# Padding the right-hand pools by 32 bytes, and asking for the next pair's halves and output splits earlier

## The chip, the cores and the metric

The kernel runs on one core of a Trainium2 chip. The metric is device time in microseconds (us) of one launch. The engines named below are PE (matrix products; it loads a stationary operand and streams a moving one past it), ACT and DVE (elementwise work, both can read the PSUM accumulators), POOL (elementwise work on SBUF) and SP, whose queue issues all the transfers here. Each engine and the SP queue work strictly in the order of their own instruction lists.

## The reference

Three layers in a row on 2304 tokens (4 batches of 576), width 512, all in float32:

```python
scores = scale * np.matmul(q, k.transpose(0, 1, 3, 2))
ret = scores * Dmat[None, :, :, :]
x = np.matmul(ret, v)                        # then heads side by side: (2304, 512)
h = x @ w_in                                 # 512 -> 2048
g = np.maximum(h, 0.0) + alpha * np.minimum(h, 0.0)
x2 = g @ w_out                               # 2048 -> 512
gate = 1.0 / (1.0 + np.exp(-(x2 @ w_gate)))  # 512 -> 1536
y = gate * (x2 @ w_val) @ w_out2             # 1536 -> 512
```

## The kernel before

Every float32 operand of a large product is split into a high and a low part (`split`: ACT writes the high part, then DVE the low part), and one product is three matmuls: high by high, high by low, low by high (`products`, line 562). A matmul of 512 columns is the unit of PE's work; "a group of 12" below is four such products, or two of the factored ones.

The tokens are cut into block 0 (256 tokens) and blocks 1 to 4 (512 each). The stages on PE's list, which is written by hand and is in program order:

- **Retention and layer 2 of block 0**, with the first `h` of block 1, up to about 152 us of the span; the weights are made from 64-bit words by ACT, DVE and POOL at the same time.
- **Layer 2 of blocks 1 to 4**, up to about 507 us: for each of 16 slices `f`, `ffn1_h` makes `h` (12 matmuls, stationary a slice of `w_in`, moving the tile `x`), ACT and DVE make `g` of it, and `ffn1_y` adds 12 matmuls into `y`. `h` has two accumulators, so `h` of slice f+2 needs `g` of slice f to be done. In block 4 the factors of pair 0 are made beside it (`left_factors(0, i)` at f = 7 and 10).
- **Layer 3 for pairs of blocks**, (1, 2) and then (3, 4): `z_step(n, t)` for t = 0 to 5 uses seven factored products (names a, b, c, e) with quarter weights `tq` as the stationary operand and factors `xf` as the moving one; each step is 14 products of 6 matmuls. Then `o_phase(n, r)` for the two blocks of the pair: 12 steps `i`, each splits one gated tile into `pp`, and multiplies it with an output weight `wo` (12 matmuls). The order of the steps is f = 0, 6, 1, 7, 2, 8, 3, 9, 4, 10, 5, 11. Pair 0's two phases make o1 and o2, pair 1's make o3 and o4. While o1 and o2 run, `left_factors(1, i)` for i = 0 and 1 makes pair 1's factors: it loads two halves `x2` (four transfers), POOL makes two sums and differences `s` of them, and seven splits make `xf1_*`.
- **Block 0 through layer 3** in plain form, from about 882 us.

The order of ACT, DVE, POOL and SP is not written by hand: a scheduler with a timeline of its own sets it, so that work which the program writes later can stand ahead of work written earlier.

Most tiles live in slots of 4096 bytes a partition, a line from which the oldest free one is taken (`slot`, `free`). Two pools lie on the right side of SBUF: `xp` (the tiles `x`, the moving operand of `h`) and, in the same place after layer 2 is done, `wide` with eight slots:

```python
xp = x_only.enter_context(tc.tile_pool(name="xp", bufs=2, side="right"))
...
pool = ctx.enter_context(tc.tile_pool(name="wide", bufs=1, side="right", reuse_waits="tile"))
spare.extend((pool, f"wide{i}") for i in range(NWIDE))
quarter_slots.extend(spare.pop() for _ in range(NQ))
```

The quarter weights have 14 slots of their own: the first seven were taken from the left side (f = 13 of block 4), the last seven are those of `wide`. They are used in turn, seven to a step, so the steps t = 0, 2, 4 read `tq` from the left side and t = 1, 3, 5 from the right. The eighth slot of `wide` goes into the common line.

Of the kernel before, what the change touches and what calls it, by code (L numbers as in the profile page):

```python
# [10 lines left out]
F32 = mybir.dt.float32  # L11
F32R = mybir.dt.float32r
# [7 lines left out]
P = 128  # L20
# [3 lines left out]
DM = 512  # L24
# [14 lines left out]
PAIRS = ((1, 2), (3, 4))  # L39
# [63 lines left out]
def retention_two_ffn(ctx: ExitStack, tc: tile.TileContext, att, cst, alpha, w1, w2, out):  # L103
    nc = tc.nc
# [8 lines left out]
    ps_a = ctx.enter_context(tc.tile_pool(name="ps_a", bufs=1, space=PSUM))  # L113


    x_only = ctx.enter_context(ExitStack())
    xp = x_only.enter_context(tc.tile_pool(name="xp", bufs=2, side="right"))
    att_only = ctx.enter_context(ExitStack())
# [16 lines left out]
    x2d = [dp.tile([P, KC, nb], F32, tag=f"x2d{j}", name=f"x2d{j}") for j, nb in enumerate(BLOCKS)]  # L135
# [9 lines left out]
    def slot(shape, dtype, name, line=spare):  # L145
        where = pool, tag = line.popleft()
        t = pool.tile(shape, dtype, tag=tag, name=name)
        held[t.tensor.name] = [where, 1, line]
        return t

    def free(t):
        h = held[t.tensor.name]
        h[1] -= 1
        if not h[1]:
            where, _, line = held.pop(t.tensor.name)
            line.append(where)
# [22 lines left out]
    def split(hi, lo, src, first=False):  # L179

        a = nc.scalar.activation(hi, src, AF.Copy)  # L181
        d = nc.vector.tensor_tensor(out=lo, in0=src, in1=hi.bitcast(F32), op=ALU.subtract)  # L182
        if first:
            urgent["act"].append(a)
            urgent["dve"].append(d)
# [55 lines left out]
    def fetch(f, m):  # L241
        if RES <= f < NF1 and (f, m) not in wt:
            wt[f, m] = slot([P, 2, DM], F32R, f"v{f}_{m}")
            uses[f, m] = 1
            nc.sync.dma_start(out=wt[f, m].bitcast(F32), in_=w1d[f, m])
# [84 lines left out]
    def second_pace(every):  # L330
        second_step()
        due[0] += 1
        if due[0] >= every:
            due[0] = 0
            begin_job()
        elif due[0] >= every - 2:
            ask()
# [164 lines left out]
    def runs_of(j):  # L502
        return [n for n, ch in enumerate(CHUNKS) if ch[0] == j]
# [6 lines left out]
    def att_stages(j):  # L510

        for n in runs_of(j):
            x_of(n)
            s_sb = att_scores(n, ps_a, "ab")
            load_qk(n + 1)
            yield
            att_values(n, s_sb, ps_a, "ab")
            load_kv(n + 1)
            if n + 1 < len(CHUNKS):
                att_q(n + 1)  # L520
                att_v(n + 1)
            yield
# [46 lines left out]
    def ffn1_h(j, f):  # L569
        w = weight(f, 0)  # L570
        nb = BLOCKS[j]
        ps = ps_h.tile([P, nb], F32, tag="h", name=f"h{j}_{f}")
        products(ps, [(cols(w, k), x_t[j][:, :, k]) for k in range(KC)])
        used(f, 0)
        t = small.tile([P, nb], F32, tag="t", name=f"t{j}_{f}", bufs=1)
        nc.scalar.activation(t, ps, AF.Relu)  # L576
        nc.scalar.activation(ps, ps, AF.Relu, scale=-1.0)  # L577
        nc.vector.scalar_tensor_tensor(ps, ps, na_sb[:, f:f + 1], t, ALU.mult, ALU.add)  # L578
        name = f"g{j}_{f}"
        g_t[j, f] = slot([P, 2, nb], F32R, name) if nb > DM // 2 else half_of_slot(name)  # L580
        split(g_t[j, f][:, 0], g_t[j, f][:, 1], ps, True)
# [41 lines left out]
    quarters = {}  # L623
    gated = {}

    def left_factors(n, i):

        a, b = [slot([P, 2, DM], F32, f"x2_{n}_{k}") for k in (i, i + 2)]
        for k, t in ((i, a), (i + 2, b)):
            for e, j in enumerate(PAIRS[n]):  # L630
                nc.sync.dma_start(out=t[:, e], in_=x2d[j][:, k, :])
        u, v = [slot([P, 2, DM], F32, f"s{n}_{i}_{c}") for c in range(2)]
        add = lambda o, x, y, op: nc.gpsimd.tensor_tensor(out=o, in0=x, in1=y, op=op)
        add(u[:, 0], a[:, 1], b[:, 1], ALU.add)
        add(u[:, 1], u[:, 0], a[:, 0], ALU.subtract)
        add(v[:, 0], a[:, 0], a[:, 1], ALU.subtract)
        add(v[:, 1], b[:, 0], u[:, 1], ALU.subtract)
        for m, src in ((1, a[:, 0]), (5, u[:, 0]), (6, u[:, 1]), (2, b[:, 0]), (7, v[:, 0]), (3, v[:, 1]), (4, b[:, 1])):
            x = factors[m, i] = slot([P, 2, DM], F32R, f"xf{n}_{m}_{i}")
            split(x[:, 0], x[:, 1], src)  # L640
        for t in (a, b, u, v):
            free(t)

    PLACE = {1: (0, 0), 5: (0, 1), 2: (1, 0), 6: (1, 1), 3: (2, 0), 7: (2, 1)}

# [2 lines left out]
    def load_quarters(t):  # L648
        need(t, 0)
        need(t, 1)  # L650
        for k in (0, 3, 1, 4, 2, 5, 6):
            w = quarters[t, k] = slot([P, 2, 2, 2, P], F32R, f"tq{t}_{k}", quarter_slots)
            nc.sync.dma_start(out=w.rearrange("p a i h j -> p a (i h j)").bitcast(F32), in_=td[t][k])
# [68 lines left out]
    def load_outer(f):  # L722
        need(f)
        outer[f] = slot([P, 2, DM], F32R, f"wo{f}")
        nc.sync.dma_start(out=outer[f].bitcast(F32), in_=wod[f])

    def second_y(ps, j, g, f, first, last):
        w = outer[f]
        for e, t in enumerate(ps):
            products(t, [(cols(g, e), w)], first, last)  # L730
            if last:
                r = FIRST[j] + e * P
                drain(e, f"ost{j}_{e}", t, out[r:r + P, :])

    ORDER2 = [f + c * NSTEP for f in range(NSTEP) for c in range(2)]

    def o_phase(n, r, between):
        j = PAIRS[n][r]
        ps = [
            pool.tile([P, DM], F32, tag=tag, name=f"o{j}_{tag}")  # L740
            for pool, tag in [(ps_y, "y")] * 2 + ([(ps_a, "a"), (ps_a, "b")] if r else [(ps_h, "h")] * 2)
        ]
        for i, f in enumerate(ORDER2):
            if i == 0:
                load_outer(ORDER2[0])
                load_outer(ORDER2[1])
            if i + 2 < NF2:
                load_outer(ORDER2[i + 2])
            g = slot([P, 2, DM], F32R, f"pp{j}_{f}")
            split(g[:, 0], g[:, 1], gated[f][:, r])  # L750
            second_y(ps, j, g, f, i == 0, i == NF2 - 1)
            free(g)
            free(outer.pop(f))
            if r:
                free(gated.pop(f))
            between(i)
# [49 lines left out]
    done = [0]  # L806
# [8 lines left out]
    def later(n):  # L815

        while len(late) > n:
            ffn1_y(*late.pop(0))
# [24 lines left out]
    n = runs_of(2)[0]  # L843
# [3 lines left out]
    for j in range(1, NBLK):  # L847
        stages = att_stages(j + 1) if j + 1 < NBLK else iter(())
        first = step1 if j == 1 else 0
        total = 2 * len(runs_of(j + 1))  # L850
        span = SPAN * (NF1 - first) // NF1
        staged = 0
        if j == NBLK - 1:

            for x in "ab":
                ps = ps_a.tile([P, DM], F32, tag=x, name=f"whole{x}")
                nc.tensor.matmul(ps, wt[0, 0][:, 0, :P], x_t[j][:, 0, 0], start=True, stop=True)
            att_only.close()
            pool = ctx.enter_context(tc.tile_pool(name="late", bufs=1, reuse_waits="tile"))
            spare.extend((pool, f"late{i}") for i in range(NLATE))  # L860
        for f in range(first, NF1):
            fetch(f, 0)
            fetch(f + 1, 0)
            fetch(f, 1)
            ffn1_h(j, f)
            if j > 1:
                second_pace(PACE_T[j == NBLK - 1])
            if j == NBLK - 1:
                if f in (7, 10):
                    left_factors(0, f // 10)  # L870
                if f == 13:
                    quarter_slots.extend(spare.popleft() for _ in range(NQ))
                    load_quarters(0)
            for point in range(2):
                if staged < total and staged * span < total * (2 * (f - first) + point):
                    next(stages)
                    staged += 1
                if point == 0:
                    later(BEHIND - 1)
            late.append((j, f))  # L880
        for _ in stages:
            pass
# [5 lines left out]
    def in_z(n, t):  # L888
# [7 lines left out]
            second_step()  # L896
        return between

    def in_o(n, r):
        def between(i):  # L900
            if n + 1 < len(PAIRS):
                if i == (1, 4)[r]:
                    left_factors(n + 1, r)
                if r == 1 and i == 6:
                    load_quarters(0)
            elif r == 1 and i == 2:
                load_x0()
        return between
# [14 lines left out]
    for f in range(NF2):  # L923
# [3 lines left out]
        g = plain_z(f, ws.pop(f))  # L927
# [51 lines left out]
```

## Time and profile before

| what | value |
|---|---|
| median of 3 runs | 940.03 us (938.67 to 940.82) |
| profiled execution, own time | 939.09 us |
| its span, first to last instruction | 937.2 us |
| PE busy | 898.6 us, 96% |
| DVE, ACT, POOL busy | 470.7, 404.9, 120.6 us |
| mean granted clock of PE | 0.989 |

The profiled execution's own time is 1.9 us over its span and 0.9 us under the median. A share is an average over the stages named above; the stretches are read one by one in the rows below. A busy PE need not be at its best rate, so the rows of equal work are compared with each other too.

### The profile page before, as it was taken

To read this page: it belongs to the slowest core of one execution; us is meant where nothing else is said; L and a number is where in the kernel's file an instruction comes from. 1 tells how busy PE (TensorE), PEld (TensorE's weight loads), DVE (VectorE), ACT (ScalarE), POOL (GpSimd) and SP (SyncE) were. 2 spreads that over 40 slices of the span, in tenths; PEclk is the share of its full clock that TensorE was granted. 3 is DMA by queue.
4 is the path that set the end of the run, shared out by engine and by line. 5 is a ranking of instruction groups with operands and counts; after the bars stand their busy time and mean duration, and the time that the engine had idled before them with its cause. 6 is when DMAs were issued, how large, how long until landed. Compare 5 with 4: busy or idle time off the path is not lost.

```text
span 937.2 us, 13173 instructions
## 1 busy us (share of the span) xinstructions
PE 898.6 (96%) x4890; PEld 744.0 (79%) x4890; DVE 470.7 (50%) x765; ACT 404.9 (43%) x772; POOL 120.6 (13%) x110
## 2 busy tenths in 40 slices
PE   6789899999999999999999999999899999999998
PEld 5678778778888888887778888887688888888897
DVE  2889985433544654468573645565332332422111
ACT  3579774334434543457565444443323222422111
POOL 6000004221100330034230100012100000000000
PEclk9799999999999999999999999999999999999999
DMA  9435786833366665588888899898727662459950
GB/s 308 159 135 175 239 310 208 275 130 104 124 213 231 208 236 180 185 275 304 303 329 312 316 402 334 284 389 326 236 98 257 184 200 70 158 199 390 379 200 23
DMA packets 74063, 219.89 MB, mean 235 GB/s; under 512 B 12048, under 2 KB 13072, under 8 KB 74000
## 3 DMA queue, kind: packets, MB, share of 16 engines
q1 hardware_dynamic: 74000, 219.05, 66.6%
q8 instruction: 39, 0.64, 0.3%
q14 instruction: 24, 0.20, 0.1%
HBM read 171.83 MB, written 47.19 MB: 234 GB/s over the span
## 4 chain that ended last, share of the span: by engine, by line
PE 70%; DVE 10%; DMA 10%; ACT 5%; issue 2%; SPq 2%; POOL 1%; ACTq 0%; DVEq 0%; POOLq 0%
PE a L562 13%; PE h L562 13%; PE y L562 13%; PE o_y L562 6%; DMA r<-w 4%; PE z L562 4%; PE e L562 3%; PE c L562 3%; PE b L562 3%; PE o_h L562 3%; PE o L562 2%; DVE r L209 2%; DVE r L212 1%; PE o_a L562 1%; PE o_b L562 1%
## 5 line engine op out<-in xcount | busy, mean ns | idle before, releaser
L562 PE MATMUL h<-x,w 128*128 128x512 f32 (+1 forms) x684 | 151.6, 372 | 12.1 <-DVE g L182 10.2
L562 PEld LDWEIGHTS h<-x,w 128*128 128x128 f32 x684 | 116.4, 191 | 37.7 <-DVE g L182 12.9
L562 PE MATMUL a<-xf,tq 128*128 128x512 f32 x576 | 138.6, 392 | 0.0
L562 PEld LDWEIGHTS a<-xf,tq 128*128 128x128 f32 x576 | 108.0, 188 | 24.4
L562 PE MATMUL y<-g,w 128*128 128x512 f32 x492 | 120.7, 394 | 0.4 <-ACT yst L596 0.4
L562 PEld LDWEIGHTS y<-g,w 128*128 128x128 f32 x492 | 92.0, 189 | 22.2 <-ACT yst L596 0.8
L578 DVE SCALAR_TENSOR_TENSOR h<-h,na_sb,t 128x512 f32<-128x512 f32 (+1 forms) x80 | 56.1, 702 | 83.1 <-ACT h L577 82.8
L562 PE MATMUL o_y<-wo,pp 128*128 128x512 f32 x288 | 74.9, 395 | 4.3 <-DVE pp L182 2.2
L576 ACT ACTIVATE t<-h 128x512 f32<-128x512 f32 (+1 forms) x80 | 44.0, 551 | 75.8 <-PE h L562 75.6
L562 PE MATMUL h<-x,v 128*128 128x512 f32 x276 | 69.1, 399 | 2.3 <-DVE g L182 2.3
L204 ACT ACTIVATE r<-r 128x512 f32<-128x512 f32 x68 | 46.0, 676 | 56.8 <-DMA r<-w 56.6
L562 PEld LDWEIGHTS o_y<-wo,pp 128*128 128x128 f32 x288 | 54.3, 190 | 16.9 <-DVE pp L182 3.1
L562 PE MATMUL y<-g,v 128*128 128x512 f32 x276 | 67.1, 392 | 0.0
L562 PEld LDWEIGHTS h<-x,v 128*128 128x128 f32 x276 | 51.1, 188 | 15.4 <-DVE g L182 3.1
L181 ACT ACTIVATE g<-h 128x512 fp32r<-128x512 f32 (+1 forms) x80 | 44.2, 553 | 44.0 <-DVE h L578 43.6
L562 PEld LDWEIGHTS y<-g,v 128*128 128x128 f32 x276 | 51.5, 188 | 11.8 <-issue 0.5
L182 DVE TENSOR_TENSOR pp<-p,pp 128x512 fp32r<-128x512 f32 x48 | 34.7, 734 | 51.0 <-ACT pp L181 51.0
L182 DVE TENSOR_TENSOR g<-h,g 128x512 fp32r<-128x512 f32 (+1 forms) x80 | 50.7, 634 | 18.9 <-ACT g L181 16.4
L263 POOL TENSOR_TENSOR r<-r,r 128x256 f32<-128x256 f32 x24 | 25.0, 1041 | 267.0 <-DVE r L212 253.0
L181 ACT ACTIVATE pp<-p 128x512 fp32r<-128x512 f32 x48 | 29.6, 628 | 58.9 <-PE o_h L562 31.9
L209 DVE CUSTOM_DVE_ANT_0 r<-r,top 128x1024 uint16<-128x1024 uint16 x68 | 49.0, 725 | 3.7 <-ACT r L205 0.7
L212 DVE SCALAR_TENSOR_TENSOR r<-r 128x512 uint32<-128x512 uint32 x68 | 48.5, 716 | 0.5
(101 smaller groups left out, 1296.1 us busy)
## 6 DMA issues: line engine op xcount, KB each, us to landing
tq<-td SPq DMA_DIRECT2D x84, 512.0 KB, 4.9
r<-w SPq DMA_DIRECT2D x68, 512.0 KB, 5.5
wo<-wod SPq DMA_DIRECT2D x60, 512.0 KB, 5.3
v<-w1d SPq DMA_DIRECT2D x46, 512.0 KB, 4.6
td<-q SPq DMA_DIRECT2D x36, 512.0 KB, 4.2
zp<-td SPq DMA_DIRECT2D x48, 256.0 KB, 5.5
kv<-att SPq DMA_DIRECT2D x16, 512.0 KB, 4.8
qk<-att SPq DMA_DIRECT2D x15, 512.0 KB, 4.8
```

What stands on the lines that cost most here:

```text
L181: a = nc.scalar.activation(hi, src, AF.Copy)
L182: d = nc.vector.tensor_tensor(out=lo, in0=src, in1=hi.bitcast(F32), op=ALU.subtract)
L204: nc.scalar.activation(high.bitcast(F32), high.bitcast(F32), AF.Copy, scale=2.0 ** -112)
L209: nc.vector.tensor_tensor(out=low.bitcast(I32), in0=low.bitcast(I32), in1=top.bitcast(I32), op=ALU.add)
L212: nc.vector.scalar_tensor_tensor(low, high, 0x80000000, low, ALU.bitwise_and, ALU.bitwise_or)
L263: sub = lambda o, a, b: nc.gpsimd.tensor_tensor(out=o, in0=a, in1=b, op=ALU.subtract)
L562: nc.tensor.matmul(ps, l, r, start=first and i == 0, stop=last and i == len(todo) - 1, skip_group_check=joins)
L576: nc.scalar.activation(t, ps, AF.Relu)
L578: nc.vector.scalar_tensor_tensor(ps, ps, na_sb[:, f:f + 1], t, ALU.mult, ALU.add)
```

## The change

Three edits. A tile of 8 float32 numbers (32 bytes) in a new pool at the right end of SBUF pushes all right-hand pools down by 32 bytes; behind it they begin at multiples of 64 bytes, before they began 32 bytes off one. The loads of the halves are cut out of `left_factors` into `load_halves` and asked for two steps ahead; for pair 1 the seven splits are no longer written at one place, but two for each step of the output phase from step 3 or 6 on, with 4 moved ahead of 7 and 3. And in `o_phase` the splits `pp` are written two steps ahead of their products and put on the list of urgent ones.

```diff
+    pad = ctx.enter_context(tc.tile_pool(name="pad", bufs=1, side="right"))
+    pad_sb = pad.tile([P, 8], F32, tag="pad", name="pad_sb")
+    nc.gpsimd.memset(pad_sb, 0.0)
     x_only = ctx.enter_context(ExitStack())
     xp = x_only.enter_context(tc.tile_pool(name="xp", bufs=2, side="right"))
...
+    halves = {}
+
+    def load_halves(n, i):
+
+        for k in (i, i + 2):
+            x = halves[k] = slot([P, 2, DM], F32, f"x2_{n}_{k}")
+            for e, j in enumerate(PAIRS[n]):
+                nc.sync.dma_start(out=x[:, e], in_=x2d[j][:, k, :])
+
     def left_factors(n, i):
 
-        a, b = [slot([P, 2, DM], F32, f"x2_{n}_{k}") for k in (i, i + 2)]
-        for k, t in ((i, a), (i + 2, b)):
-            for e, j in enumerate(PAIRS[n]):
-                nc.sync.dma_start(out=t[:, e], in_=x2d[j][:, k, :])
+        a, b = halves.pop(i), halves.pop(i + 2)
         u, v = [slot([P, 2, DM], F32, f"s{n}_{i}_{c}") for c in range(2)]
...
-        for m, src in ((1, a[:, 0]), (5, u[:, 0]), (6, u[:, 1]), (2, b[:, 0]), (7, v[:, 0]), (3, v[:, 1]), (4, b[:, 1])):
+        done = {6: u, 4: b, 3: v, 7: a}
+        for m, src in ((1, a[:, 0]), (5, u[:, 0]), (6, u[:, 1]), (2, b[:, 0]), (4, b[:, 1]), (7, v[:, 0]), (3, v[:, 1])):
             x = factors[m, i] = slot([P, 2, DM], F32R, f"xf{n}_{m}_{i}")
             split(x[:, 0], x[:, 1], src)
-        for t in (a, b, u, v):
-            free(t)
+            if m in done:
+                free(done[m])
+            yield
...
-            g = slot([P, 2, DM], F32R, f"pp{j}_{f}")
-            split(g[:, 0], g[:, 1], gated[f][:, r])
+            for f2 in ORDER2[i + 2 * (i > 0):i + 3]:
+                g = parts[f2] = slot([P, 2, DM], F32R, f"pp{j}_{f2}")
+                split(g[:, 0], g[:, 1], gated[f2][:, r], True)
+            g = parts.pop(f)
             second_y(ps, j, g, f, i == 0, i == NF2 - 1)
...
+                if f in (5, 8):
+                    load_halves(0, f // 8)
                 if f in (7, 10):
-                    left_factors(0, f // 10)
+                    for _ in left_factors(0, f // 10):
+                        pass
...
+    under_left = []
+
     def in_o(n, r):
         def between(i):
             if n + 1 < len(PAIRS):
                 if i == (1, 4)[r]:
-                    left_factors(n + 1, r)
+                    load_halves(n + 1, r)
+                if i == (3, 6)[r]:
+                    under_left.append(left_factors(n + 1, r))
+                for g in under_left:
+                    next(g, None), next(g, None)
```

PE's list is the same in both kernels, instruction by instruction. What moves is the order on the other engines. In the names below `pp1_7` is the split of gated tile 7 for o1, `xf1_5_0` the factor 5 of pair 1 for i = 0, `w2_5_2` an output weight being made, `x2_1_k` a half and `s1_*` a sum; the last number is a running number of the tile.

**First place:** DVE's list in o1, before the change, up to the low parts of `pp1_7` and `pp1_8` (steps 3 and 5 of the phase).

```order
L182 TENSOR_TENSOR xf1_2_0_5680<-x2_1_2_5660,xf1_2_0_5680 128x512
L182 TENSOR_TENSOR xf1_1_0_5671<-x2_1_0_5659,xf1_1_0_5671 128x512
L223 TENSOR_TENSOR w2_5_2_5603<-r2_5_2_5569,w2_5_2_5603 128x512
L223 TENSOR_TENSOR w2_11_2_5613<-r2_11_2_5600,w2_11_2_5613 128x512
L182 TENSOR_TENSOR pp1_2_5728<-p0_2_4998,pp1_2_5728 128x512
L182 TENSOR_TENSOR xf1_5_0_5674<-s1_0_0_5665,xf1_5_0_5674 128x512
L182 TENSOR_TENSOR pp1_7_5711<-p0_7_4843,pp1_7_5711 128x512
L182 TENSOR_TENSOR xf1_6_0_5677<-s1_0_0_5665,xf1_6_0_5677 128x512
L182 TENSOR_TENSOR pp1_8_5745<-p0_8_4999,pp1_8_5745 128x512
```

The same place after the change; `pp1_7` and `pp1_2` stand before this piece.

```order
L186 TENSOR_TENSOR pp1_3_5724<-p0_3_5157,pp1_3_5724 128x512
L186 TENSOR_TENSOR pp1_8_5695<-p0_8_5004,pp1_8_5695 128x512
L227 TENSOR_TENSOR w2_5_2_5608<-r2_5_2_5574,w2_5_2_5608 128x512
L186 TENSOR_TENSOR pp1_9_5747<-p0_9_5158,pp1_9_5747 128x512
L227 TENSOR_TENSOR w2_11_2_5618<-r2_11_2_5605,w2_11_2_5618 128x512
L186 TENSOR_TENSOR xf1_4_0_5762<-x2_1_2_5673,xf1_4_0_5762 128x512
L186 TENSOR_TENSOR xf1_2_0_5742<-x2_1_2_5673,xf1_2_0_5742 128x512
L186 TENSOR_TENSOR pp1_4_5770<-p0_4_5311,pp1_4_5770 128x512
L186 TENSOR_TENSOR xf1_5_0_5719<-s1_0_0_5710,xf1_5_0_5719 128x512
```

The splits for steps 3 to 7 of o1 now stand ahead of the first factor that reads a half, and those for steps 0 to 8 ahead of the first one that reads a sum of POOL's.

**Second place:** DVE's list in o2 before the change, up to `pp2_8` (step 5).

```order
L182 TENSOR_TENSOR pp2_2_5946<-p0_2_4998,pp2_2_5946 128x512
L182 TENSOR_TENSOR xf1_2_1_5982<-x2_1_3_5962,xf1_2_1_5982 128x512
L182 TENSOR_TENSOR xf1_4_1_5991<-x2_1_3_5962,xf1_4_1_5991 128x512
L182 TENSOR_TENSOR xf1_1_1_5973<-x2_1_1_5961,xf1_1_1_5973 128x512
L182 TENSOR_TENSOR xf1_5_1_5976<-s1_1_0_5967,xf1_5_1_5976 128x512
L182 TENSOR_TENSOR pp2_8_5996<-p0_8_4999,pp2_8_5996 128x512
```

After the change, from step 4's split on:

```order
L186 TENSOR_TENSOR pp2_2_5923<-p0_2_5003,pp2_2_5923 128x512
L598 COPY ost1_0_5854<-o1_y_5623 128x512
L186 TENSOR_TENSOR pp2_5_6063<-p0_5_5465,pp2_5_6063 128x512
L598 COPY ost1_2_5865<-o1_h_5625 128x512
L186 TENSOR_TENSOR pp2_3_5957<-p0_3_5157,pp2_3_5957 128x512
L186 TENSOR_TENSOR pp2_8_5940<-p0_8_5004,pp2_8_5940 128x512
L186 TENSOR_TENSOR pp2_4_5997<-p0_4_5311,pp2_4_5997 128x512
L186 TENSOR_TENSOR xf1_1_1_6018<-x2_1_1_5972,xf1_1_1_6018 128x512
L186 TENSOR_TENSOR xf1_5_1_6021<-s1_1_0_6012,xf1_5_1_6021 128x512
```

The first factor of i = 1 now stands behind the splits for steps 0 to 8 of o2 (`pp2_9` and `pp2_1` stand ahead of this piece); before, four factors stood ahead of step 5's.

**Third place:** DVE's list in block 4 of layer 2 before the change, from the `h` of slice 7 to the `g` of slice 7.

```order
L578 SCALAR_TENSOR_TENSOR h4_7_4116<-h4_7_4116,na_sb_85,t4_7_4129 128x512
L182 TENSOR_TENSOR xf0_1_1_4330<-x2_0_1_4318,xf0_1_1_4330 128x512
L182 TENSOR_TENSOR g4_7_4133<-h4_7_4116,g4_7_4133 128x512
```

The same after the change:

```order
L582 SCALAR_TENSOR_TENSOR h4_7_4127<-h4_7_4127,na_sb_90,t4_7_4140 128x512
L277 TENSOR_TENSOR q4_0_1_4322<-r2_4_0_4066,q4_0_1_4322 128x4x128
L186 TENSOR_TENSOR xf0_3_1_4353<-s0_1_1_4330,xf0_3_1_4353 128x512
L186 TENSOR_TENSOR xf0_6_1_4341<-s0_1_0_4329,xf0_6_1_4341 128x512
L186 TENSOR_TENSOR xf0_2_1_4344<-x2_0_3_4239,xf0_2_1_4344 128x512
L186 TENSOR_TENSOR g4_7_4144<-h4_7_4127,g4_7_4144 128x512
```

Three factors of pair 0 for i = 1, two of which read POOL's sums, now stand ahead of `g4_7`; slices 8 to 11 have fewer ahead of theirs than before.

## Rows read from the trace of the kernel before

**Rows 1.** The page: busy time, share of the span and instructions by engine.
```profile
PE 898.6 (96%) x4890; PEld 744.0 (79%) x4890; DVE 470.7 (50%) x765; ACT 404.9 (43%) x772; POOL 120.6 (13%) x110
```

**Rows 2.** Stretches: from:to length, PE busy (instructions), granted clock, DMA share, GB/s.
```profile
152.00:412.00 260.00, 258.88 (x1599) 1.00 0.59 197
412.00:507.00 95.00, 90.74 (x389) 1.00 0.82 295
507.00:628.30 121.30, 121.30 (x530) 1.00 0.94 346
628.30:700.50 72.20, 67.92 (x289) 0.98 0.63 228
816.40:882.00 65.60, 65.60 (x290) 1.00 0.84 310
```

**Rows 3.** The chain that ended last, layer 2 of block 4: start, us, what.
```profile
484.91 2.80 PE h L562 x12
487.71 2.75 PE y L562 x12
```

**Rows 4.** The chain, groups of 12 in the steps t = 0 and 1.
```profile
515.26 2.72 PE e L562 x12
...
534.39 2.80 PE e L562 x12
```

**Rows 5.** The chain, sixes in o1.
```profile
652.62 1.36 PE o_h L562 x6
653.98 1.40 PE o_y L562 x6
```

**Rows 6.** Stretches, instructions on tiles h alone; columns as in rows 2.
```profile
152.00:412.00 260.00, 113.55 (x455) 1.00 0.59 197
412.00:507.00 95.00, 47.89 (x192) 1.00 0.82 295
```

**Rows 7.** Timeline of PE in o1, o2: start, us, what, [idle before and releaser].
```profile
637.78 1.21 PE L562 MATMUL o_y<-wo,pp 128*128 128x512 f32 x4 [0.70 <-DVE pp L182]
...
677.88 0.73 PE L562 MATMUL o_y<-wo,pp 128*128 128x512 f32 x2 [2.03 <-ACT pp L181]
680.14 2.07 PE L562 MATMUL o_y<-wo,pp 128*128 128x512 f32 x4 [1.54 <-DVE pp L182]
682.01 1.49 PE L562 MATMUL o_a<-wo,pp 128*128 128x512 f32 x3
```

**Rows 8.** Timeline of all engines, o1.
```profile
629.65 4.57 POOL L633 TENSOR_TENSOR s<-x,x 128x512 f32<-128x512 f32 x1 [91.88 <-DMA x<-x2d]
...
635.94 1.78 DVE L182 TENSOR_TENSOR pp<-p,pp 128x512 fp32r<-128x512 f32 x1
```

**Rows 9.** Timeline of all engines, o2 (SPq is the transfer queue).
```profile
670.30 0.85 SPq L631 DMA_DIRECT2D x<-x2d  x2
...
674.88 1.76 POOL L633 TENSOR_TENSOR s<-x,x 128x512 f32<-128x512 f32 x1 [36.00 <-DMA x<-x2d]
...
678.34 1.75 DVE L182 TENSOR_TENSOR pp<-p,pp 128x512 fp32r<-128x512 f32 x1
```

**Rows 10.** Transfers issued from 600 to 700 us: count, size, median us to landing.
```profile
wod<-w SPq DMA_DIRECT2D x5, 512.0 KB, 7.9
x<-x2d SPq DMA_DIRECT2D x8, 256.0 KB, 6.8
```

**Rows 11.** Timeline of PE, block 4: the last two of five waits.
```profile
472.62 3.06 PE L562 MATMUL h<-x,v 128*128 128x512 f32 x12 [1.60 <-DVE g L182]
...
479.13 3.06 PE L562 MATMUL h<-x,v 128*128 128x512 f32 x12 [0.70 <-DVE g L182]
```

**Rows 12.** Timeline of DVE and of POOL, block 4.
```profile
464.49 0.69 DVE L182 TENSOR_TENSOR g<-h,g 128x512 fp32r<-128x512 f32 x1
...
476.19 1.74 POOL L633 TENSOR_TENSOR s<-x,s 128x512 f32<-128x512 f32 x1
```

**Rows 13.** Waits of PE, whole span: us in total, times, longest.
```profile
PE h L562 <- DVE g L182: 12.5, 12, 2.4
```

More of the change, by code (lines that the diff above doesn't have):

```diff
@@ L742, in o_phase @@
         ]
+        parts = {}
         for i, f in enumerate(ORDER2):
```

## The prediction

> **What bounds the kernel.** I read the page first: PE is busy for 96% of the span [rows 1], so only two things can be worth much, PE's idle time and the rate of its matmuls. The stretches say where the idle time lies: PE has next to none in layer 2 from 152 to 412 us, none in the steps of pair 0, none in pair 1's output phases, 4.3 us in block 4 (95.00 less 90.74) and 4.3 us in pair 0's output phases (72.20 less 67.92) [rows 2]. The list of PE's waits names DVE's `g` for block 4 and the first stage [rows 13]; the change leaves the weights' work of the first stage alone, so I leave that stage out.
>
> Then the chain, for the rate. Where it runs along PE, its pieces are PE's own pace, because matmuls follow each other without a gap. Twelve matmuls of 512 columns take 2.72 us in the step t = 0 and 2.80 in t = 1 [rows 4]; `h` takes 2.80 and `y` beside it 2.75 [rows 3]; in o1 a piece of six takes 1.36, and here and there 1.40 [rows 5]. The operands differ in one thing that I can find: the slow ones read one operand from a right-hand tile (`x` as the moving operand of `h`; `tq` of odd steps as the stationary one; in the output phases whatever sits in the eighth slot of `wide`). So a right-hand operand, moving or stationary, costs 0.08 us per twelve, 6.7 ns per matmul.
>
> **The pad.** It moves every right-hand tile by 32 bytes, to a multiple of 64. Nothing on the left moves by it, and all of the fast pieces read only there. I take the start address as the cause and price each place at the full 0.08 us:
> - `h` from 152 to 412 us: 455 instructions [rows 6] are 38 groups of 12, PE has no slack there, so 38 x 0.08 = 3.0 us.
> - `h` of block 4: 192 instructions, 16 groups. From 438 to 482 us PE waits for `g` anyway [rows 11], so a faster `h` there only waits longer; I count half, 8 x 0.08 = 0.6 us.
> - odd steps: three in each pair, 84 matmuls each, 42 groups: 42 x 0.08 = 3.4 us. PE is never idle in the steps [rows 2], though transfers keep the DMA engines at 0.94 there.
> - the output phases: about ten sixes at 1.40 instead of 1.36 over all four, 0.4 us.
>
> Sum 7.4 us. Bounds: 0 if the address is not the cause; 9.5 if the other half of block 4 (0.6) and the 0.03 by which `y` is over 2.72 beside `h` (54 groups, 1.6) go too. I take 7.4, since moving and stationary operands, in four places of the program, show the same 6.7 ns. The pad's fill of 8 columns goes on POOL ahead of a fill of 512 that is there already, while the first loads are under way; I price it at nothing.
>
> The Trainium skill, "SBUF — State Buffer", section Specifications (TRN2), speaks against this: it gives SBUF lines of 16 bytes, with a penalty for each crossing to a new line. By that rule a shift of 32 bytes, two whole lines, changes no crossing, and the term would be 0 and the sum 932.4 us. No row here shows a line's length; the rows show only that the right-hand operands are the slower ones.
>
> **The output splits and the halves.** Pair 0's two phases take 72.20 us, and pair 1's, with the same 288 matmuls, 65.60 [rows 2]. The rows between show where the 6.6 us go. In o1, step 3 waits 0.70 us for the low part of `pp1_7` [rows 7]. On DVE it stands behind `xf1_5_0`, and that behind POOL's first sum, which started at 629.65, when its half had landed, and took 4.57 us [rows 8]; `pp1_7` is done at 637.72. In o2, step 5 waits 2.03 and then 1.54 us for `pp2_8` [rows 7], which stands behind four factors of i = 1; the second half's transfers were issued at 670.30, POOL started at 674.88, and `pp2_8` came off DVE at about 680.1 [rows 9]. After that pause PE is slow for a while: the next four matmuls take 2.07 us, where a third of 2.72 would be 0.91, and the next three 1.49 [rows 7]; the granted clock of the stretch is 0.98 [rows 2], so for part of it PE ran at 1.2 GHz and not at 2.4. Waits 4.27, slow clock about 1.8, refilling after each pause the rest.
>
> After the change the splits of steps 3 to 7 stand ahead of any factor in o1. The loads are no earlier: on SP's list the four transfers stand about three places later than before, since they now wait for slots that PE frees. That is harmless if what stands behind them is due late. The first split behind a half is `pp1_4`, for step 8: due 8 x 2.72 = 21.8 us after 628.3, at 650. A half that lands a whole transfer later than 629.65, by 6.8 us [rows 10], still leaves 13 us. The first split behind a sum is `pp1_10`, step 9, due at 652.8. The sum's tile takes the slot of a weight that is just being stored, so add 7.9 us [rows 10]: 629.65 + 7.9 + 4.57, 1.76 for the second sum and two splits come to 645, and 7 us are left. In o2 `pp2_8` no longer stands behind factors but takes the slot of a stored output tile: issued at about the phase's start, landed within 8 us, due 13.6 us after the start. Behind the sums comes `pp2_10`, due 24.5 us after the start (661); the first sum ended at 676.6 in the old run, 15.6 after it. So both waits go, nothing new ends last, and PE has no reason to slow down: 6.6 us. Bounds: 0 if the old waits only move, 6.6.
>
> **Block 4.** The work for pair 0's factors stays the same, its order changes. Before, the last two waits come when slices 8 and 9 have factors and a raw weight ahead of their `g` [rows 11]. After, `g4_7` has three factors ahead of it, two behind POOL's sums, whose last one started at 476.19 in the old run [rows 12]; but slices 8 to 11 have fewer. `g4_7` ended at 465.2 [rows 12], and PE's `h` of slice 9 could start at once, so it had no margin. I expect one wait more at slice 9, of about 3 us, and most of the 4.3 us gone elsewhere: in sum 0. Bounds: -4.3 if all waits go, +4 if a second one of 3 to 4 us comes.
>
> **The sum.** 939.09 (the profiled execution's own time: span 937.2 and 1.9 around it) - 7.4 - 6.6 + 0 = 925.1. The median of the runs is 0.9 above that execution, which would give 926.0; I forecast 925.5.
>
> **Rivals.**
> 1. The pad does nothing: the top of SBUF is slower as a place, or the rate hangs on another thing that right-hand tiles share. For it: no tile in the trace lies there with another address. Against it: moving and stationary operands lose the same. Time: 939.1 - 6.6 = 932.5.
> 2. The waits of the output phases move instead of going: SP's list holds the transfers of o1's results, of the halves and of `wo` in one row, and a `wo` late for a step makes PE pause and slow down as at 680 us. One such pause cost 3.6 us idle and 1.8 of slow clock [rows 7], so 925.5 + 5.4 = 930.9. Against it: the margins above, the least 5 us.
> 3. PE's gain is lost in pair 0's steps, where the DMA engines are at 0.94 [rows 2] and a step that is 0.56 us shorter asks for the same bytes: three odd steps, 1.7 us, 927.2. Against it: each `tq` slot is refilled a step ahead.
> 4. Slower than before: block 4's `g` behind the late halves. Each `g` that waits for a landing of 6.8 us and sums [rows 10, 12] stops PE two slices later; five slices from 5 to 9 have factors ahead of them. It decides from 14 us of new waits on, some four slices at 3.5 us each, and gives 941 to 943. Against it: old waits there are 1.6 us at most [rows 11], and DVE has the same work.
>
> **How the numbers follow.** My forecast 0.72 (it includes the third rival, 0.06 of it), the first rival 0.10, the second 0.12, the fourth 0.03; the remaining 0.03 for both terms failing without new waits, about no change. The likeliest case alone reaches from 920.5 (all of block 4's waits gone) to 929 (a second wait there). For the range I go up to 932, which takes in most of the second rival and leaves out half of the first and the slower cases: 920 to 932. A measurement of this kernel can tell about 0.2%, 1.9 us, from no change: faster 0.94, the same 0.03, slower 0.03.
>
> **What would show it.** Right: in the chain, `h` and odd steps at 2.72 per twelve, no six at 1.40; no wait of PE on `pp` between 612 and 700 us and a granted clock of 1.00 there; the two phases of pair 0 in 65 to 66 us. Wrong: `h` still at 2.80 (first rival), a wait on `wo` or `pp` in o1 or o2 (second), PE's waits on `g` in block 4 well above 4.3 us (fourth).

## The result and the profile after

| | before | after |
|---|---|---|
| median | 939.35 us (937.81 to 940.82, 4 runs) | 930.61 us (930.14 to 931.73, 4 runs) |
| ratio | | 0.9909, 95% interval 0.9889 to 0.9929 |
| profiled execution: span | 937.2 us | 930.0 us |

Faster, by 0.9%. The forecast was 925.5 us, in a range of 920 to 932. So the sign and the range held, and the middle was 5 us too low. Where the 7.2 us between the two spans arose is read from the starts of the matmuls that open each stage:

| stage | before, us | after, us | difference | forecast |
|---|---|---|---|---|
| first stages and layer 2, to block 4 | 412.14 | 412.75 | +0.6 | -3.0 |
| block 4 | 94.79 | 95.57 | +0.8 | -0.6 (pad), 0 (waits) |
| pair 0's steps | 121.36 | 120.24 | -1.1 | -1.7 |
| o1 and o2 | 72.21 | 65.31 | -6.9 | -6.6 and some of the 0.4 of the sixes |
| pair 1's steps | 115.93 | 115.42 | -0.5 | -1.7 |
| o3 and o4 | 65.54 | 65.43 | -0.1 | the rest of the 0.4 |
| to the end | 55.25 | 55.24 | 0.0 | 0 |

The output phases came out as forecast, and nearly everything that the pad should have given is missing. The stretches of the kernel after, columns as in [rows 2] (length, PE busy, granted clock, DMA share, GB/s):

```profile
152.00:412.00 260.00, 258.77 (x1596) 1.00 0.56 195
412.00:508.00 96.00, 91.65 (x390) 0.98 0.81 298
508.00:628.70 120.70, 120.70 (x532) 1.00 0.93 348
628.70:694.00 65.30, 65.30 (x290) 1.00 0.69 255
```

The last row answers to 72.20 with 67.92 busy in [rows 2]: PE has no idle time left in o1 and o2, and the clock stays at 1.00. In the first row nothing has moved: PE is as busy as before with the same `h` and `y`. The chain that ended last says why (start, us, what):

```profile
502.94 2.80 PE h L566 x12
505.73 2.74 PE y L566 x12
...
516.63 2.72 PE e L566 x12
...
535.70 2.75 PE e L566 x12
```

`h` still takes 2.80 as in [rows 3]; the odd steps went from the 2.80 of [rows 4] to 2.75, not to 2.72. In pair 1's even steps there is even a new slow place, again from the chain:

```profile
704.90 2.72 PE a L566 x12
707.62 2.78 PE c L566 x12
...
726.89 2.80 PE c L566 x12
```

The last line is the same group in an odd step, where the others take 2.75. This is why pair 1's steps gave only 0.5 where pair 0's gave 1.1: in the program as built, the factor 3 of i = 0, which half of the products of `c` read, now sits in the eighth slot of `wide`, on the right. With the pad alone, where no factor lies on the right, `c` takes 2.72 and 2.75 and pair 1's steps give 1.1 too.

In o1 the splits `pp` no longer stand behind sums. Timeline of DVE and of POOL there (start, us, what, idle time before):

```profile
630.99 1.29 DVE L186 TENSOR_TENSOR pp<-p,pp 128x512 fp32r<-128x512 f32 x2
...
637.58 1.84 POOL L643 TENSOR_TENSOR s<-x,x 128x512 f32<-128x512 f32 x1 [98.68 <-DMA tq<-td]
...
642.49 1.74 POOL L643 TENSOR_TENSOR s<-x,s 128x512 f32<-128x512 f32 x1
```

POOL starts 7.9 us later than in [rows 8], which is the delay that the prediction allowed for. The trace puts the wait down to a load of `tq`, which came last; in the program as built the sum takes the slot of a weight (`w2_10_2`) whose store was issued at 628.90, as the prediction had it. The last sum ends at 644.2. The low part of `pp1_10`, the first split behind a sum, is done at 644.8, where the prediction had 645; PE needs it at 653.1 and does not wait.

In block 4, the timeline of PE and then that of DVE:

```profile
452.98 3.06 PE L566 MATMUL h<-x,w 128*128 128x512 f32 x12 [0.82 <-DVE g L186]
...
467.87 4.35 PE L566 MATMUL h<-x,w 128*128 128x512 f32 x12 [3.53 <-DVE g L186]
472.02 3.21 PE L566 MATMUL y<-g,w 128*128 128x512 f32 x12
```

```profile
465.33 1.28 DVE L186 TENSOR_TENSOR xf<-s,xf 128x512 fp32r<-128x512 f32 x2
466.53 0.68 DVE L186 TENSOR_TENSOR xf<-x,xf 128x512 fp32r<-128x512 f32 x1
467.13 0.68 DVE L186 TENSOR_TENSOR g<-h,g 128x512 fp32r<-128x512 f32 x1
```

`g_7` ends at 467.8 behind three factors, 2.6 us later than in [rows 12], and `h` of slice 9 waits 3.53 for it; the waits of [rows 11] are gone, one of 0.82 is left. Those twelve matmuls take 4.35 and the next 3.21, where 2.96 and 2.90 are usual in this view: about 1.7 us lost to a slower pace behind the pause, at a granted clock of 0.98 over the stretch. The waits themselves add up to 4.35 us, against 4.26 before.

### The profile page after: what moved, and what is told of

The parts are those of the page before. It is cut to its first block, busy times and chain, and to the rows that moved or that the text cites. A ratio compares the mean times of both kernels' runs of the same rounds, so it can differ in the third digit from the quotient of the medians.

```text
span 930.0 us, 13173 instructions
## 1 busy us (share of the span) xinstructions
PE 893.7 (96%) x4890; PEld 742.7 (80%) x4890; DVE 470.1 (51%) x765; ACT 406.2 (44%) x772; POOL 118.0 (13%) x111
## 4 chain that ended last, share of the span: by engine, by line
PE 68%; DMA 10%; DVE 10%; ACT 5%; issue 3%; SPq 2%; POOL 2%; ACTq 0%; DVEq 0%; POOLq 0%
PE a L566 14%; PE h L566 10%; PE y L566 10%; PE o_y L566 7%; DMA r<-w 5%; PE z L566 4%; PE c L566 4%; PE b L566 4%; PE e L566 4%; PE o_h L566 4%; DVE r L213 2%; PE o L566 2%; PE o_b L566 2%; PE o_a L566 2%; DVE r L216 1%
```

## The experiments

Two questions: what the pad should have done and did not, and which of the other two parts removed the waits. The first seven kernels are about the first one. The table has the time of each, that of the kernel before on the same chip, and the span of its profile; "both parts" are the earlier halves and the output splits two steps ahead.

| kernel | us (runs) | before | ratio, 95% interval | span |
|---|---|---|---|---|
| pad 32 alone | 933.82 (12) | 936.12 | 0.9981, 0.9954 to 1.0008 | 936.9 |
| both parts, no pad | 931.96 (12) | 936.12 | 0.9963, 0.9939 to 0.9987 | 929.9 |
| both parts, pad 96 | 930.65 (12) | 936.12 | 0.9939, 0.9916 to 0.9961 | 928.6 |
| both parts, pad 224 | 926.06 (6) | 936.12 | 0.9888, 0.9855 to 0.9921 | 924.0 |
| the same, left moved by 128 | 933.33 (10) | 937.22 | 0.9964, 0.9939 to 0.9990 | 931.8 |
| both parts, pad 160 | 932.37 (1) | 936.50 | a single run, no interval | 930.6 |
| pad 224 alone | 931.59 (10) | 936.50 | 0.9938, 0.9912 to 0.9965 | 929.7 |
| pad 224, output splits alone | 932.22 (7) | 937.22 | 0.9941, 0.9917 to 0.9964 | 929.6 |
| pad 224, halves alone | 934.43 (10) | 937.22 | 0.9961, 0.9938 to 0.9985 | 929.0 |
| pad 224, both, pair 0's halves late | 925.67 (4) | 936.50 | 0.9886, 0.9855 to 0.9917 | 926.6 |
| pad 224, both, factors spread in block 4 | 925.09 (4) | 937.22 | 0.9860, 0.9811 to 0.9910 | 923.5 |
| the changed kernel again | 930.10 (8) | 936.03 | 0.9929, 0.9903 to 0.9954 | 929.5 |

Runs of one kernel scatter by several us here. In the profiles the scatter lies ahead of block 4, whose start moves between 408.1 and 414.0 us, and in block 4; the steps of both pairs and their output phases repeat to 0.05 us where kernels have the same work, and what comes after them to about 0.1. So the stages, and the pace in them, decide more than the spans.

### Pad 32 alone

```diff
+    pad = ctx.enter_context(tc.tile_pool(name="pad", bufs=1, side="right"))
+    pad_sb = pad.tile([P, 8], F32, tag="pad", name="pad_sb")
+    nc.gpsimd.memset(pad_sb, 0.0)
```

(on the kernel before)

> The kernel before with the 32-byte pad alone; all engines keep the order of before. Theory (the pad is worth only what odd steps and the eighth slot gain): odd steps at 2.75 per twelve instead of 2.80, h still at 2.80, the waits on pp in o1 and o2 as before; 42 x 0.05 + 0.3 = 2.4 us less, about 937. Rival (the gains of the two edits overlap, so that the pad alone gives nothing that can be measured): 939.4, within 0.7 of before.

Measured: no difference that can be told from none. Its chain:

```profile
502.40 2.80 PE h L565 x12
...
535.53 2.76 PE e L565 x12
```

The waits on `pp` of [rows 7] are all there (the two longest, 1.01 and 1.54), and o1 and o2 take 72.95. Pair 0's steps are 0.8 us shorter and pair 1's 1.1. So the pad of the change moves only the odd steps.

### Both parts without a pad

```diff
-    pad = ctx.enter_context(tc.tile_pool(name="pad", bufs=1, side="right"))
-    pad_sb = pad.tile([P, 8], F32, tag="pad", name="pad_sb")
-    nc.gpsimd.memset(pad_sb, 0.0)
```

(on the changed kernel)

> The changed kernel without its pad; all engines keep the order of the changed kernel. Theory: odd steps back at 2.80, no wait on pp in o1 and o2, pair 0's two phases in 65.6 us, block 4 with its one long wait at slice 9: 939.4 - 6.6 + 0.8 = 933.6 less up to 0.5. Rival (the pad is what took the waits away, by a shift in time): waits on pp back, about 938.

Measured: `h` and odd steps at 2.80, as before; no wait on `pp`, o1 and o2 in 65.36. The gain in the output phases belongs to the other parts wholly. In block 4 the long wait is at slice 9 again:

```profile
467.38 3.06 PE L563 MATMUL h<-x,w 128*128 128x512 f32 x12 [3.54 <-DVE g L183]
```

It is as long as in the first profile of the changed kernel, but no slower pace follows, and block 4 takes 94.04 where it took 95.57.

### Pads of 96 and of 224 bytes

```diff
-    pad_sb = pad.tile([P, 8], F32, tag="pad", name="pad_sb")
+    pad_sb = pad.tile([P, 24], F32, tag="pad", name="pad_sb")
```

(and 56 in place of 24)

With 96 the right-hand tiles begin at 128 modulo 256, with 224 at 0 modulo 256. In the programs as built, the slots on the left begin at 0 modulo 256 in all kernels so far; the right-hand tiles of the kernel before begin at 224, those of the changed kernel at 192. The start of the moving operand less that of the stationary one, modulo 256, called the distance below, is then 224 for `h` and 32 for the odd steps before, and 192 and 64 after.

> The changed kernel with a pad of 96 bytes, so that right-hand pools begin at multiples of 128 (and 128 off a multiple of 256). Theory A (the pace hangs on the start address of either operand, and 128 is what counts): h 2.72 and odd steps 2.72 per twelve; 38 x 0.08 + 42 x 0.03 + 0.6 and up to 1.6 by y, so 924 to 926. Theory B (moving operands care about a larger multiple, 256): odd steps 2.72 or 2.75, h 2.80, 929 to 930.6. Theory C (h is slow by its place or its pattern, not by its address): odd steps 2.72, h 2.80, 929.4.

> The changed kernel with a pad of 224 bytes: right-hand pools begin at multiples of 256, as all left-hand slots do. Theory A: the same as with 96 bytes, 924 to 926. Theory B: 924 to 926 here only. Theory C: h still 2.80, 929.4. Rival to all three: the right side is slower as a place, and odd steps stay at 2.75, 930.6.

Chain with 96:

```profile
499.79 2.79 PE h L566 x12
502.58 2.73 PE y L566 x12
...
532.60 2.79 PE e L566 x12
```

Chain with 224:

```profile
498.88 2.72 PE h L566 x12
501.60 2.72 PE y L566 x12
...
531.54 2.72 PE e L566 x12
```

A multiple of 128 is no better for `h` than one of 64 and worse for the odd steps; a multiple of 256 puts every group at 2.72, `y` beside `h` too. Against the version without a pad the median falls by 5.9 us, and so does the span.

### Left-hand slots moved by 128 bytes

```diff
+    shift_sb = const.tile([P, 32], F32, tag="shift", name="shift_sb")
+    nc.gpsimd.memset(shift_sb, 0.0)
```

(on the version with 224)

> The version with a pad of 224 bytes, with one more small tile on the left, so that all slots of `wide` but the eighth begin at 128 modulo 256 while the right-hand tiles stay at 0 modulo 256. If each operand's own start address counts (theory B), nearly every matmul of layer 2 now has at least one operand off: `y` and the even steps go from 2.72 to between 2.75 and 2.80 per twelve, `h` (stationary from the left, moving from the right) and the odd steps too; some 200 groups of twelve at 0.05 to 0.08 give 10 to 16 us, so 936 to 942 beside 926 without the shift. If only the distance between the two operands counts, `y` and the even steps (both operands left) stay at 2.72, and `h` and the odd steps alone are slow: some 96 groups at 0.05 to 0.08, 5 to 8 us, so 931 to 934. If the right-hand side is special and 256 merely moved it, nothing changes: 926.

The slots that move are those of the common line, on the left; of `wide`, whose slots are on the right, none moves. Chain:

```profile
500.64 2.73 PE y L568 x12
503.37 2.79 PE h L568 x12
...
517.06 2.72 PE e L568 x12
...
536.18 2.79 PE e L568 x12
```

`y` and the even steps, whose two operands now both begin at 128, keep 2.73 and 2.72; `h` and the odd steps, with one at 128 and one at 0, are slow. So theory B of these expectations, that each operand's own start counts, falls: the distance between the two counts.

### Right-hand tiles at 64 modulo 256

`pad_sb` with 40 columns. The sign of the distance tells two theories apart.

> The version with a pad, made 160 bytes, so that right-hand tiles begin at 64 modulo 256 and left slots at 0. The runs so far put the pace on the distance between moving and stationary operand, modulo 256: 0 gave 2.72 per twelve, 128 gave 2.79, and the changed kernel gave 2.80 where moving less stationary is 192 (`h`) and 2.75 where it is 64 (odd steps). If the distance with its sign decides, the two change places here: `h` 2.75, odd steps 2.80. If the kind of operand decides (a right-hand `x` of `h` costs 0.08, a right-hand `tq` less), they stay as in the changed kernel: `h` 2.80, odd steps 2.75. Even steps 2.72 in both. Time 928 to 931 in both; the pieces of the chain decide.

```profile
501.38 2.76 PE h L566 x12
504.14 2.77 PE y L566 x12
...
515.07 2.72 PE e L566 x12
...
534.19 2.80 PE e L566 x12
```

`h` and odd steps change places with the changed kernel, as the sign has it. But `y` rose to 2.77, which nothing foresaw, so that `h` and `y` together take 5.53 against 5.54 in the changed kernel and 5.44 at distance 0: in layer 2 no other distance that was tried saves anything worth having. What the chip does with the two addresses is not shown by these runs; only the pace is.

### Pad 224 alone

The pad of 56 columns on the kernel before.

> The kernel before with nothing but the pad of 224 bytes: both operands of every matmul with the same start modulo 256. If the pad's worth is the pace alone, `h` and odd steps go from 2.80 to 2.72 and the time falls by the 6 us that the same step gave in the version with the other parts: 930 to 932, with the waits on `pp` of [rows 7] still there. The rival, that a faster layer 2 and faster steps only run into transfers that are no earlier, has pieces at 2.72 but more waits (on `tq`, `wo` or `g`), and 934 to 937.

Chain, then the longest wait on `pp` in PE's timeline:

```profile
497.93 2.72 PE h L565 x12
...
530.57 2.72 PE e L565 x12
```

```profile
674.44 1.20 PE L565 MATMUL o_y<-wo,pp 128*128 128x512 f32 x4 [1.55 <-DVE pp L185]
```

The ratio, 0.9938, is that of a gain of 5.8 us. o1 and o2 take 71.91, and pair 0's steps 119.68 with PE busy throughout (expected of the pace: 121.36 - 21 x 0.08 = 119.68). So the pad's gain and that of the other parts add up, and no transfer takes the faster pace back.

### One of the two other parts at a time

Output splits alone (on the version with 224), pair 1's lines; pair 0's halves are late as well, by the edit shown under Block 4:

```diff
-                if i == (3, 6)[r]:
-                    under_left.append(left_factors(n + 1, r))
-                for g in under_left:
-                    next(g, None), next(g, None)
+                    for _ in left_factors(n + 1, r):
+                        pass
```

Halves alone:

```diff
-            for f2 in ORDER2[i + 2 * (i > 0):i + 3]:
-                g = parts[f2] = slot([P, 2, DM], F32R, f"pp{j}_{f2}")
-                split(g[:, 0], g[:, 1], gated[f2][:, r], True)
-            g = parts.pop(f)
+            g = slot([P, 2, DM], F32R, f"pp{j}_{f}")
+            split(g[:, 0], g[:, 1], gated[f][:, r])
```

> The version with a pad of 224 bytes, but halves loaded right ahead of their sums and all seven splits of the factors written in one place, as before; the output splits alone stand two steps ahead. By the prediction's account of pair 0's phases, `pp1_7` and `pp2_8` were late because of what stood ahead of them on DVE, and the splits two steps ahead take them past it: the phases then stay near 65.5 us without the halves' part, or a wait on `pp` of under 1 us is left, since in o1 the splits of steps 3 to 5 stand behind sums again: 926 to 928. The rival, that the earlier halves are what removed the waits, has a wait of 1 to 4 us on `pp` in o1 or o2 here, and 69 to 72 us for the phases: 930 to 933. In block 4 four waits on `g` of 1.6 us at most each, as [rows 11], in place of one of about 4.

> The version with a pad of 224 bytes, with halves loaded two steps ahead of their sums and factors split two at a time, but each output split in its own step, as before. If the halves and the spread factors are enough, no wait on `pp` is left in o1 and o2 and they take 65 to 66 us: 926. If the splits two steps ahead are what removed the waits, a split that stands behind POOL's first sum (of 4.57 us in the old trace) or behind two factors is late by 1 to 3 us in each of the two phases, and the phases take 68 to 72 us: 929 to 933. Block 4 is as with both parts, one wait on `g` of about 4 us.

Neither theory foresaw what came. Waits of PE in o1 and o2 with the splits alone:

```profile
640.11 1.66 PE L566 MATMUL o_y<-wo,pp 128*128 128x512 f32 x6 [1.05 <-DMA wo<-wod]
683.82 1.62 PE L566 MATMUL o_y<-wo,pp 128*128 128x512 f32 x6 [2.60 <-DMA wo<-wod]
```

and with the halves alone:

```profile
643.32 2.93 PE L566 MATMUL o_y<-wo,pp 128*128 128x512 f32 x6 [5.29 <-DMA wo<-wod]
```

No wait on `pp` is left with either part, but a weight `wo` is late, and the phases take 69.51 and 72.65 (neither part: 71.91; both: 65.28). The chain of the halves alone follows the weight back:

```profile
626.84 1.78 DVE w L227
628.61 0.75 DVE xf L186
...
631.52 0.61 DVE w L227
...
632.15 5.38 DMA wod<-w
...
637.55 5.73 DMA wo<-wod
```

The last part `w` of an output weight stands on DVE behind factors, the store of that weight waits for it at the head of SP's list, and the loads `wo` queue behind the store. The order of the change, shown above under the change, has `w2_5_2` ahead of every factor; with one part undone the factors come first again. So each part alone trades the waits on `pp` for one on `wo`, which is the second rival's mechanism, and only together do they pay.

### Block 4

Pair 0's halves late again:

```diff
-                if f in (5, 8):
-                    load_halves(0, f // 8)
                 if f in (7, 10):
+                    load_halves(0, f // 10)
```

Factors two per slice (`under_left` is made ahead of block 4 for it):

```diff
-                    for _ in left_factors(0, f // 10):
-                        pass
+                    under_left.append(left_factors(0, f // 10))
+                for g in under_left:
+                    next(g, None), next(g, None)
```

> The version with a pad of 224 bytes, but pair 0's halves in block 4 asked for right ahead of their sums (slices 7 and 10), as before; the output phases keep both their parts. If the earlier halves are what put three factors ahead of `g_7` and so made the wait of about 4 us at slice 9, that wait goes back to several of 1 to 2 us, and block 4 is shorter by 0 to 1 us: 925 to 926. If the wait comes from the work itself, one of 3 to 4 us stays, somewhere in slices 8 to 11. The output phases stay at 65.3 us in both.

> The version with a pad of 224 bytes, with pair 0's factors in block 4 also split two at a time, over slices 7 to 13, in place of seven at once behind each sum. If the wait of PE on `g` at slice 9 comes from the row of splits ahead of `g_7` on DVE, it falls from about 4 us to under 1, and the slow clock after it goes too: block 4 shorter by 3 to 4 us, 922 to 923. If it comes from POOL's sums, that is from the late halves alone, the wait stays at 3 to 4 us and the time at 926; if the factors, now later, make the first step of pair 0 wait, a wait on a factor of 1 to 3 us shows at about 500 us and the time is 925 to 928.

With the halves early and the factors in one piece (pad 224), PE waits 4.09 us at slice 7 and 0.28 at slice 9; these expectations put the long wait at slice 9, where it is in the first profile of the changed kernel. With the halves late:

```profile
447.97 3.01 PE L566 MATMUL h<-x,w 128*128 128x512 f32 x12 [1.56 <-DVE g L186]
...
477.82 4.61 PE L566 MATMUL h<-x,v 128*128 128x512 f32 x12 [1.88 <-DVE g L186]
```

The long wait is back to small ones, in slices 6, 10 and 11, as the first theory had it, and block 4 takes 94.50 where it took 94.06: the early halves cost and save nothing there. With the factors spread, PE waits 0.55 at slice 9 and not at slice 7, and block 4 takes 88.38, but the gain is handed back at its end (PE's timeline, then the chain):

```profile
503.49 2.93 PE L566 MATMUL a<-xf,tq 128*128 128x512 f32 x6 [2.45 <-DVE g L186]
```

```profile
495.92 5.04 DMA r<-w
...
501.04 0.65 ACT r L208
501.69 0.54 ACT r L209
502.23 0.49 ACT g L185
```

The last `g` stands on ACT behind an output weight `r` whose transfer lands at 501, and the next six products take 2.93 where 1.52 is usual in this view. Pair 0's steps take 123.87 in place of 119.71, so of 5.7 us 1.5 remain, which the medians (925.09 and 926.06) do not tell apart. It was not a factor that came late, as the expectation had it, but a transfer in ACT's way.

### The changed kernel again

Unaltered, for a second ratio beside those with the pad of 224.

> The changed kernel itself, unaltered, for a second ratio. The three versions with right-hand tiles at multiples of 256 and both other parts gave 0.986 to 0.989 of the kernel before, and the changed kernel 0.9909 in its first comparison. If the 256 bytes are worth the 6 us that the stages show (from 94 to 95.5 us in block 4, 119.7 to 120.2 in pair 0's steps, 114.2 to 115.4 in pair 1's, and `h` in layer 2), the changed kernel lies at 0.991 to 0.995 here, 928 to 932. If the difference is only scatter of the first stage, it lies at 0.987 to 0.990 like the other three, 924 to 927.

0.9929 (0.9903 to 0.9954), inside the first band of these expectations. The three versions with both parts and a pad of 224 have 0.9888, 0.9886 and 0.9860, on three chips; the intervals of the first two end at 0.992, so they overlap with this one, and it is the stages that say more: 119.7 against 120.24 in pair 0's steps (but for the spread factors, whose 123.87 has the wait shown above) and 114.24 against 115.42 in pair 1's, every time. In block 4 the long wait was at slice 7 here:

```profile
455.87 4.61 PE L566 MATMUL h<-x,w 128*128 128x512 f32 x12 [2.56 <-DVE g L186]
```

At slice 9 it waited 0.19. The block took 93.93, so the 0.8 us of the first comparison there is scatter: the same list of work makes PE wait for `g_5` in one execution and for `g_7` in another.

## Why the prediction was right, and where it was wrong

**What bounds it**: right. PE's pace and PE's idle time were the two things to be had, and both moved.

**The pad, -7.4**: this step failed, and it is the whole of the miss. It took the start address as the cause, which the pads of 96 and 224 and the moved left side bear out, but it also took it that a multiple of 64 would be as good as where the fast operands lie. No row of before told 64 from 256, since all fast operands lay at multiples of 256. What counts, in these groups, is the distance between the two operands modulo 256, and the change only took it from 224 to 192 for `h` and from 32 to 64 for the odd steps. Term by term: `h` up to block 4 3.0, measured none (2.80 stays); `h` of block 4 0.6, none; odd steps 3.4, measured 1.6 (1.1 and 0.5); the sixes 0.4, measured 0.1 in o3 and o4. The sizes were right for a pad that reaches distance 0: with 224, pair 0's and pair 1's steps lose 1.68 and 1.69, together the 3.4 of the working, and against no pad the whole is worth 5.9 us where 7.4 and at most 9.5 stood. By the lines of 16 bytes of the Trainium skill, "SBUF — State Buffer", section Specifications (TRN2), no pad here would matter; the trace differs: 0.08 us per twelve between distances of 224 and 0.

That the time still fell in the range is in part luck: a term of 7.4 gave 1.7, and the range reached up to 932 for the sake of the second rival, not of this failure: the 932.5 that goes with a pad worth nothing lay outside it.

**The output phases, -6.6**: right, measured 6.9 with 0.0 of PE's idle time and the clock at 1.00. The margins held, with `pp1_10` done at 644.8 where 645 was worked out. That this agrees so closely is luck: the first sum took 1.84 and not the 4.57 counted, and the operations of DVE beside the sums took longer than counted (the low part of `pp1_10` 1.73, where 0.69 is usual). What the step did not see is that it hangs on both parts together. It named `pp` as what stood behind factors and sums; a weight's `w` stood there as well, and would have been late next.

**Block 4, 0**: right. One wait of about 3 us came (3.53 at slice 9 in the first profile, 2.56 at slice 7 in the second) and most of the rest went; that it must be `g_7`'s was right in one profile of two. The step left out the slower pace behind such a pause, 1.7 us in the first profile; without the pad the same pause had none, so the +0.8 is inside the scatter.

**The first stages** gave +0.6, which no step foresaw and which is scatter: kernels with the same work there start block 4 between 408.1 and 414.0.

The profiled execution took 931.73 us. From 925.1, 5.7 less from the pad, 0.8 and 0.6 of scatter and 0.3 more from the output phases give 931.9. Three figures of the working are slightly off, and nothing hangs on them: the bound 9.5 (its terms add up to 9.6), the 932.4 without the pad (932.5), and the 920.5 with all of block 4's waits gone (925.1 less 4.3 is 920.8).

**The rivals.** The first, that the pad does nothing, was nearly what happened (932.5), but not for its reason: the place is not slow, the distance was still wrong. The second, waits that move on to `wo`, did not come to pass in the change, and came with either part alone. The third is out: at 2.72 in every step (pad 224) PE stays busy through 120 of 120 us with the DMA engines at 0.93. The fourth is out: 4.35 us of waits in block 4, not 14.

## What to carry to other kernels

Where matmuls of one shape have two paces, sort them by where their operands start, moving less stationary, modulo 256 bytes, and take the padding all the way to a difference of 0 before judging it; a smaller step can give nothing. When work is moved off the head of an engine's list, look for everything that stood behind it, the slow store's input too, since a repair of one wait can make a transfer's issue the next. And a time that agrees within its range can still hide a term that gave nothing: compare by stage.

## What the runs showed of the hardware that was not expected

The pace of a 128x512 fp32r matmul stream depends on the distance between the starts of the two operands. Per twelve, moving less stationary modulo 256: 0 gives 2.72 us, 128 gives 2.79, 192 and 224 give 2.80, and so does 32 (odd steps of the kernel before); 64 gives 2.75 in the odd steps of the changed kernel and 2.76 in `h` with the pad of 160. No other distance was tried.

This holds where all moving operands of a group begin alike, and all stationary ones. It does not settle mixed groups: in pair 1's odd steps of the changed kernel six of the twelve matmuls of `c` have both operands at 192, a distance of 0, and six have 64, and the group takes 2.80, more than either alone would. Nor does it cover `y`: with both operands on the left, it takes 2.73 to 2.77 between slow `h` and 2.72 between fast ones. Behind the slow odd steps of the kernel before, the even ones are at 2.72 again. What makes the difference was not tried.

Operations of DVE stretch while POOL computes. From the timeline of the halves alone:

```profile
622.82 0.69 DVE L216 SCALAR_TENSOR_TENSOR r<-r 128x512 uint32<-128x512 uint32 x1
...
624.63 1.73 POOL L643 TENSOR_TENSOR s<-x 128x512 f32<-128x512 f32 x1
625.14 1.77 DVE L216 SCALAR_TENSOR_TENSOR r<-r 128x512 uint32<-128x512 uint32 x1
```

The same operation takes 0.69 when it begins ahead of the sums and 1.77 beside one. Three such in a row, of 1.77, 1.78 and 1.78, put what stood behind them on DVE off by 3.3 us, the weight of the late `wo` among it. Not every operation stretched; what tells them apart was not tried.
